# First batch's first DFT on quarters of the TensorE array, its input in halves from two queues, and a new order around it

## The chip, the cores and the metric

The kernel runs on one core of one Trainium2 chip. The metric is the device time of one execution in microseconds (us). Before the change it was 2508.93 us, the median of three runs (2508.61 to 2509.11).

## What is computed

The input x holds 8 batches of 3008 time steps by 256 channels. Each batch goes through a real FFT over time, a complex linear layer with biases, a soft threshold and the inverse FFT. Every time step then goes through a feed-forward block with a hidden width of 2048.

```
X = np.fft.rfft(x, axis=1)
Yr = Xr @ w_r - Xi @ w_i + b_r
Yi = Xr @ w_i + Xi @ w_r + b_i
Y  = sign(Y) * max(abs(Y) - 0.01, 0)
y  = np.fft.irfft(Y, n=3008, axis=1)
h  = y @ w_in
out = (h - tanh(h)) @ w_out
```

## The kernel before, in words

3008 is 64 times 47, so the FFT is done as two short DFTs by matmul: a **first DFT** over 47 points for each of 64 residues, and a **second DFT** over the 64 residues. Between the two the data goes through DRAM (`a_dram`), because the second needs rows of all residues together. After the linear layer and the threshold an inverse DFT over 64 points is written to DRAM (`z_dram`) and read back for the last inverse DFT of 47 points, which `Wave.time` does. The feed-forward block (`Chunk.up`, `Chunk.down`) then runs in 48 chunks of time steps. Batches 1 to 7 are transformed in the gaps of the feed-forward work of the batch ahead of them. Only batch 0 has nothing to hide behind, so the program begins with a stretch in which it is transformed alone. Everything below lies in this stretch.

**First DFT of batch 0** (class `Forward`). x comes in eight chunks of 96 partitions by 4 pairs of residues by 256 channels (384 KB), issued on the SP queue (L262). A chunk holds two residues one above the other, so 94 rows are in use; the rest of the 128 partitions is set to zero on POOL (L261), and the constant `f1` is block diagonal. Each chunk has two matmuls of 128 by 128 by 512 columns in float32 (L269), 16 in all. Each result is copied from PSUM to `st` by ACT or DVE in turn (L281). The 32 rows that the first units need go to DRAM first (`store_near`, L286), the other 64 later (`store_far`, L290).

**Second DFT to inverse DFT of batch 0** (class `WholeSpectrum`). There are 12 units, u0 to u11, of two frequencies each. A unit reads its rows from DRAM (L360), is transformed (L378), copied by ACT (`xf`, L477), summed by DVE (`sum`, `sf`, L482), multiplied with the linear layer (`cross`, L490 and L500; `cross_apart` for u11, L510 and L512), blended (`y`, L429), thresholded (L523, L527, L540) and inverted (L548). The units run as a software pipeline: pass i of a loop holds the transform of unit i, the cross products of unit i-1, the threshold of unit i-2 and the inverse of unit i-3.

**The weights of the linear layer** (`load_linear`, L142 to L149) are read between chunks 5 and 6 of x and combined on DVE and POOL (L155 to L165). The cross products need the result. **The feed-forward weights** come as 64-bit words and are taken apart into floats on DVE, ACT and POOL, in blocks. Six blocks, b0 to b5, are spread over the passes of the loop by two tables, `on_act` and `on_dve`, and each has steps named `exponent`, `mantissa`, `ends`, `fraction`, `scale`, `value` and `parts`.

**Filling** matmuls on zeros (`keep_warm`, L699) run ahead of the first DFT (8) and behind it (25).

The order on each engine is the order in which the program is written. Transfers of all queues take eight counters in turn, called DMAHW0 to DMAHW7 in the rows below. A transfer waits on its issuing engine until the one that took its counter before, eight transfers earlier, has landed.

Of the kernel before, what the change touches and what calls it, by code (L numbers as in the profile page):

```python
# [10 lines left out]
F32 = mybir.dt.float32  # L11
# [6 lines left out]
NP, NJ, GB = 32, 24, 5  # L18
# [14 lines left out]
def dft_constants():  # L33
# [6 lines left out]
    for par in range(2):  # L40
        plain[47 * par:47 * par + 47, 48 * par:48 * par + 48] = one
    by_pair = plain.reshape(94, 4, NJ // 2, 2).transpose(0, 2, 1, 3).reshape(94, 96)
    f1 = np.zeros((128, 2, 128))
    for half in range(2):
        f1[32 * half:32 * half + 94, half, :96] = by_pair
    f1 = f1.reshape(128, 256)
    f1s = np.zeros((94, 2, 48))
# [30 lines left out]
@with_exitstack  # L78
def spectral_ffn(ctx, tc, x, w_r, w_i, b_r, b_i, w_in, w_out, x_twice, b_turned, f1, f1s, f2, i1, i2, out):
    nc = tc.nc  # L80
# [58 lines left out]
    def load_linear():  # L139
        wr = ffn.tile([P, 2, D], F32, name="wr_f", tag="g_h")  # L140
        wi = load.tile([P, 2, D], F32, name="wi_f", tag="at", bufs=3)
        nc.sync.dma_start(out=wr, in_=w_r.rearrange("(t p) e -> p t e", p=P))  # L142
        nc.sync.dma_start(out=wi, in_=w_i.rearrange("(t p) e -> p t e", p=P))
        rows = load_bias(work.tile([33, 2, D], F32, name="bias_rows", tag="tmp", bufs=4), 33)
        return wr, wi, rows

    def load_bias(dst, n):
        for k, v in enumerate((b_r, b_i)):
            nc.sync.dma_start(out=dst[:, k, :], in_=v.rearrange("(o e) -> o e", o=1).to_broadcast([n, D]))  # L149
        return dst  # L150

# [86 lines left out]
    PAIRED, LOOK = 1, 4  # L238
    NEAR = 32
    stack = {}  # L240

    class Forward:
        def __init__(self, b, ch):
            self.b, self.ch = b, ch
            self.x, self.ps = {}, {}

        def load(self):
            if self.ch == 0:
                if self.b < PAIRED:
                    a_dram[self.b] = [dram.tile([NP, n, D], F32, name=f"a_{n}") for n in (NEAR, 96 - NEAR)]  # L250
                else:
                    a_dram[self.b] = dram.tile([2 * NP, 96, D], F32, name=f"a_{self.b}", tag="a_two")
            pool, tag = (load, "xt")
            if self.b == 0:
                pool, tag = ((load, "xt"), (load, "zin"), (work, "yh"), (work, "yl"))[self.ch // 2]
            elif self.ch >= 2:
                pool, tag = ((work, "yh"), (work, "yl"))[self.ch - 2]
            self.xt = pool.tile([P if self.b == 0 else 96, XC, D], F32, name="xt", tag=tag)
            lo = 32 * (self.ch % 2) if self.b == 0 else 0
            if self.b == 0:  # L260
                nc.gpsimd.memset(self.xt[:32] if lo else self.xt[96:], 0.0)  # L261
            nc.sync.dma_start(out=self.xt[lo:lo + 96], in_=x[self.b, :, self.ch * XC:(self.ch + 1) * XC, :])  # L262

        def whole(self, q):
            k, m = (P, P) if self.b == 0 else (94, 96)
            self.ps[q] = ps_f.tile([P, 512], F32, name="ps_f1", tag="f")
            pv = self.ps[q][:m].rearrange("p (a d) -> p a d", d=D)
            lo = self.ch % 2 * P
            nc.tensor.matmul(pv, stack["whole"] if self.b else f1f[:, lo:lo + m], self.xt[:k, 2 * q:2 * q + 2, :], start=True, stop=True)  # L269

        def keep(self, q, copy=nc.scalar.copy):
            n = 2 if self.b and self.ch >= 2 else XC
            if n == 2:
                self.st = ffn.tile([96, 2, D], F32, name="st", tag=("th", "g")[q])
            elif q == 0:
                pool, tag = (work, "st")
                if self.b == 0 and self.ch >= 2:
                    pool, tag = ((load, "xt"), (load, "zin"), (work, "yh"))[self.ch // 2 - 1]
                self.st = pool.tile([96, XC, D], F32, name="st", tag=tag)
# [4 lines left out]
        def store_near(self, q=0, n=XC):  # L284
            p = self.ch * XC + 2 * q
            nc.sync.dma_start(out=a_dram[0][0][p:p + n].rearrange("a r d -> r a d"), in_=self.st[:NEAR, 2 * q:2 * q + n])  # L286

        def store_far(self):
            p = self.ch * XC
            nc.sync.dma_start(out=a_dram[0][1][p:p + XC].rearrange("a r d -> r a d"), in_=self.st[NEAR:])  # L290

# [46 lines left out]
    def rows(parts, jp):  # L338
        late = 8 * jp >= NEAR
        t = parts[late].rearrange("a (q g e) d -> a q g (e d)", g=4, e=2)  # L340
        return t[:, jp - late * NEAR // 8]

# [347 lines left out]
    with tc.manual_schedule(engines={E.PE, E.Activation, E.DVE, E.Pool, E.SP}):  # L690
        zero = cvt.tile([P, 512], F32, name="zero", tag="w_f")
        nc.vector.memset(zero, 0.0)
# [3 lines left out]
        def keep_warm(n):  # L696
            idle = ps_h.tile([P, 512], F32, name="idle", tag="h")
            for _ in range(n):
                nc.tensor.matmul(idle, warm[:, :P], warm, start=True, stop=True)  # L699
# [4 lines left out]
        f1f = load_whole(f1, [P, 2 * P], "f1")  # L704
        first = [Forward(0, ch) for ch in range(NP // XC)]
# [5 lines left out]
        steps = [(f, q) for f in first for q in range(XC // 2)]  # L711
        for i in range(len(steps) + 1):
            if i < len(steps):
                steps[i][0].whole(steps[i][1])
            if i >= 1:
                f, q = steps[i - 1]
                f.keep(q, nc.vector.tensor_copy if i % 2 == 0 else nc.scalar.copy)
                if f is first[-1]:
                    f.store_near(q, 2)
                elif q == 1:  # L720
                    f.store_near()
                    if 4 <= f.ch < 7:
                        first[f.ch - 4].store_far()
# [24 lines left out]
        def unit(i):  # L748
# [66 lines left out]
        u11.threshold()  # L815
        for op in (b4.scale, b5.fraction, b5.scale):
            op()
# [17 lines left out]
        forward(0)  # L835
        forward(1)
        for k in range(5):
            keep(k)
            forward(k + 2)
            if k == 1:  # L840
# [7 lines left out]
        b4.value()  # L848
        keep(5)
        following[2].store()  # L850
        b5.value()
        keep(6)
        following[3].store()
        b4.parts()
        b5.parts()
        p, q = blocks[:2]
# [154 lines left out]
```

## Time and profile before

| | |
|---|---|
| median of three runs | 2508.93 us |
| profiled execution, its own time | 2506.88 us |
| its span in the trace | 2505.1 us |
| PE busy | 2488.9 us (99% of the span) |
| PEld busy | 2232.6 us (89%) |
| DVE busy | 1864.7 us (74%) |
| ACT busy | 1511.9 us (60%) |
| POOL busy | 114.5 us (5%) |

The span runs from the first to the last instruction, and the profiled execution is 1.78 us longer than it. PE's share is an average: filling matmuls on zeros count as busy too, and in the first 100 us PE waits for other work in several places.

### The profile page before, as it was taken

Reading aid. Unit: us, or ns where it says so; the run is one execution under the profiler, and the core shown is the slowest. Engines: PE = TensorE matmul, PEld = TensorE weight load, DVE = VectorE, ACT = ScalarE, POOL = GpSimd, SP = SyncE. Lnnn points to the kernel's source line nnn. Section 1 sums busy time; section 2 is a strip of 40 time slices with the busy share of each in tenths; the row PEclk is TensorE's granted clock in tenths of the full one; section 3 lists DMA queues with packets and bytes.
Section 4 is the critical chain, followed back from the end, with each engine's and each line's share of the span. In section 5 each row is a group of like instructions: output and inputs, shape, how many; then the busy total and the mean of one; then the engine's idle time right before and its main releaser. Section 6 shows DMA issues by size and latency. Waiting matters only on the chain.

```text
span 2505.1 us, 36438 instructions
## 1 busy us (share of the span) xinstructions
PE 2488.9 (99%) x13330; PEld 2232.6 (89%) x13330; DVE 1864.7 (74%) x3411; ACT 1511.9 (60%) x2930; POOL 114.5 (5%) x116
## 2 busy tenths in 40 slices
PE   9999999999999999999999999999999999999999
PEld 6789998999989999899988999889998899988888
DVE  5896887677776777777777777767777677765655
ACT  4676558555685556855577555775557655555554
POOL 2110000000001000010000000000000000000000
PEclk9999999999999999999999999999999999999999
DMA  8544227332363223633146221553216522010000
GB/s 245 180 113 127 76 68 209 90 76 62 85 188 88 70 59 90 190 80 79 43 138 165 71 74 40 152 152 78 67 39 169 133 69 63 28 51 17 20 17 17
DMA packets 156446, 236.57 MB, mean 94 GB/s; under 512 B 12498, under 2 KB 107498, under 8 KB 156266
## 3 DMA queue, kind: packets, MB, share of 16 engines
q1 hardware_dynamic: 144937, 213.78, 29.4%
q0 software_dynamic: 11328, 20.45, 5.4%
q8 instruction: 105, 1.72, 0.3%
q14 instruction: 76, 0.61, 0.1%
HBM read 138.77 MB, written 95.42 MB: 93 GB/s over the span
## 4 chain that ended last, share of the span: by engine, by line
PE 91%; DVE 5%; DMA 1%; ACT 1%; issue 1%; SPq 0%; DVEq 0%; ACTq 0%
PE o L667 37%; PE h L634 37%; PE ps_v L398 4%; PE ps_i L590 4%; PE ps_f L378 3%; PE ps_t L398 2%; PE ps_f L318 2%; DVE y L429 1%; PE ps_i L445 1%; PE ps_i L446 1%; PE ps_i L444 1%; DVE gl L654 1%; DVE g L648 1%; DMA xt<-in_x 1%; DMA xt<-in_x_twice 1%
## 5 line engine op out<-in xcount | busy, mean ns | idle before, releaser
L648 DVE TENSOR_TENSOR g<-h,th 128x502 f32<-128x502 f32 (+2 forms) x768 | 520.4, 678 | 289.1 <-ACT th L645 283.1
L645 ACT ACTIVATE th<-h 128x502 f32<-128x502 f32 (+2 forms) x768 | 452.0, 589 | 448.2 <-PE h L634 443.6
L654 DVE TENSOR_TENSOR gl<-g,gh 128x502 fp32r<-128x502 f32 (+2 forms) x768 | 524.0, 682 | 257.2 <-ACT gh L651 246.7
L651 ACT CAST gh<-g 128x502 fp32r<-128x502 f32 (+2 forms) x768 | 469.7, 612 | 356.2 <-DVE g L648 354.2
L667 PE MATMUL o<-gh,wout_l 128*128 128x502 f32 (+2 forms) x1536 | 584.9, 381 | 0.6 <-DVE ot L684 0.2
L667 PE MATMUL o<-gl,wout_h 128*128 128x502 f32 (+2 forms) x1536 | 576.9, 376 | 0.6
L667 PE MATMUL o<-gh,wout_h 128*128 128x502 f32 (+2 forms) x1536 | 576.3, 375 | 0.0
L634 PE MATMUL h<-yh,win_l 128*128 128x502 f32 (+2 forms) x1536 | 454.2, 377 | 1.4 <-DVE g L648 0.9
L634 PE MATMUL h<-yl,win_h 128*128 128x502 f32 (+2 forms) x1536 | 450.6, 375 | 0.0
L634 PE MATMUL h<-yh,win_h 128*128 128x502 f32 (+2 forms) x1536 | 450.2, 375 | 0.0
L634 PEld LDWEIGHTS h<-yh,win_l 128*128 128x128 f32 x1536 | 287.6, 188 | 44.0 <-DVE g L648 4.9
L667 PEld LDWEIGHTS o<-gl,wout_h 128*128 128x128 f32 x1536 | 289.7, 189 | 38.6 <-DVE gl L654 3.4
L634 PEld LDWEIGHTS h<-yl,win_h 128*128 128x128 f32 x1536 | 290.1, 189 | 34.8 <-DVE yl L626 0.4
L634 PEld LDWEIGHTS h<-yh,win_h 128*128 128x128 f32 x1536 | 290.2, 189 | 34.3
L667 PEld LDWEIGHTS o<-gh,wout_l 128*128 128x128 f32 x1536 | 290.7, 189 | 31.0 <-DVE ot L684 2.7
L667 PEld LDWEIGHTS o<-gh,wout_h 128*128 128x128 f32 x1536 | 290.8, 189 | 28.0
L365 POOL DMA_DIRECT2D at<-a x84 | 80.0, 1031 | 1873.1 <-DMA at<-a 931.5
L429 DVE TENSOR_TENSOR y<-tb,ps_v 64x256 f32<-64x256 f32 x384 | 160.2, 417 | 6.1 <-ACT tb L516 2.2
L313 DVE TENSOR_TENSOR xs<-xt,xs 47x512 fp32r<-47x512 f32 x208 | 138.4, 681 | 25.8 <-ACT xs L312 24.1
L312 ACT CAST xs<-xt 94x512 fp32r<-94x512 f32 x208 | 125.6, 625 | 6.4 <-DMA xt<-in_x_twice 6.3
L321 ACT COPY st<-ps_f 96x512 f32<-96x512 f32 x208 | 116.1, 579 | 1.4 <-PE ps_f L318 1.3
L625 ACT CAST yh<-yt 128x470 fp32r<-128x470 f32 (+36 forms) x200 | 87.0, 460 | 49.4 <-DVE yt L606 29.3
(113 smaller groups left out, 2488.9 us busy)
## 6 DMA issues: line engine op xcount, KB each, us to landing
xt<-in_x_twice SPq DMA_DIRECT2D x104, 384.0 KB
a<-st SPq DMA_DIRECT2D x104, 384.0 KB
at<-a SPq DMA_DIRECT2D x96, 256.0 KB
z<-zo SPq DMA_DIRECT2D x93, 240.0 KB
zin<-z SPq DMA_DIRECT2D x46, 480.0 KB
at<-a POOLq DMA_DIRECT2D x72, 256.0 KB, 5.0
out<-ot SPq DMA_DIRECT2D x29, 502.0 KB
turn<-in_i SPq DMA_DIRECT2D x96, 128.0 KB
```

What stands on the lines that cost most here:

```text
L312: nc.scalar.copy(out=xs, in_=src)
L313: nc.vector.tensor_tensor(out=xs[:47], in0=src[:47], in1=xs[:47].bitcast(F32), op=ALU.subtract)
L321: nc.scalar.copy(out=self.st[:, 2 * q:2 * q + 2, :], in_=ps[:96].rearrange("p (a d) -> p a d", a=2))
L398: nc.tensor.matmul(paired(dst, D), lhs[:, t], in_turn(rhs[:, t, :]), start=n == 0, stop=n == 5)
L429: nc.vector.tensor_tensor(out=y[ri * 64:(ri + 1) * 64, jj, :], in0=common(jj, ri), in1=self.side(ri)[jj * 64:(jj + 1) * 64], op=ALU.add,)
L590: nc.tensor.matmul(ps[:, at:at + m], self.zt[:m, k, t * P:(t + 1) * P], i2t[:m, turn:turn + m], start=True, stop=True,)
L634: nc.tensor.matmul(paired(h, n), lhs[:, t, f * P:(f + 1) * P], moving(rhs[:, t], n), start=k == 0, stop=k == 5,)
L645: nc.scalar.activation(out=th[:, :n], in_=h[:, :n], func=AF.Tanh)
L648: nc.vector.tensor_tensor(out=g[:, :n], in0=h[:, :n], in1=th[:, :n], op=ALU.subtract)
L651: nc.scalar.copy(out=gh[:, :n], in_=g[:, :n])
L654: nc.vector.tensor_tensor(out=gl[:, :n], in0=g[:, :n], in1=gh[:, :n].bitcast(F32), op=ALU.subtract)
L667: nc.tensor.matmul(paired(self.o[t], n), lhs[:, f, t * P:(t + 1) * P], in_turn(rhs[:, :n]), start=f == 0 and k == 0, stop=f == NF - 1 and ...
```

## The change

The first DFT of batch 0 gets a class of its own, `First`, and x of batch 0 a tensor of its own, `x_first`, with the two residues of a pair apart. A chunk goes to partitions 0 to 47 by SP's queue and to partitions 64 to 111 by ACT's queue. Each chunk has four matmuls of 47 rows by 64 columns of weights by 512 columns, each on another quarter of the array; 32 in all in place of 16. ACT copies the results of one half of the rows, DVE of the other. The zeros on POOL are gone. `f2` and the weights of the linear layer are read by ACT's queue, the latter behind its copies of the DFT. The near and far stores become 16 each, of half the size. Three units read their rows ahead of the far stores, not two. In the last pass the sum of u11 is put ahead of the threshold of u9, and steps of b4 and b5 move from the loop to behind it.

```diff
+    class First:
...
+            for h, queue in enumerate((nc.sync, nc.scalar)):
+                queue.dma_start(out=self.xt[64 * h:64 * h + 48], in_=x_first[h, :, self.ch * XC:(self.ch + 1) * XC, :])
+
+        def dft(self):
+            self.ps = [ps_f.tile([P, 512], F32, name="ps_f1", tag="f") for _ in range(2)]
+            for h, q in ((0, 0), (1, 1), (0, 1), (1, 0)):
+                rows = slice(64 * h, 64 * h + 47)
+                out = self.ps[h][64 * q:64 * q + 64].rearrange("p (a d) -> p a d", d=D)
+                nc.tensor.matmul(out, f1t[rows], self.xt[rows, 2 * q:2 * q + 2, :], start=True, stop=True)
+
+        def keep(self):
...
+            for h, copy in enumerate((nc.scalar.copy, nc.vector.tensor_copy)):
+                copy(out=self.st[:, :, h], in_=self.ps[h].rearrange("p (a d) -> p a d", d=D))
+
+        def store(self, part):
+            lo, hi = ((0, NEAR), (NEAR, 48))[part]
+            for q in range(2):
+                n = self.ch * XC + 2 * q
+                dst = a_dram[0][part][n:n + 2].rearrange("a h r d -> r (a h) d")
+                nc.sync.dma_start(out=dst, in_=self.st[64 * q + lo:64 * q + hi].rearrange("r a h d -> r (a h) d"))
...
-        keep_warm(8)
+        keep_warm(7, zero[:, :P], zero[:, :P])
...
-            if f.ch == 6:
-                lin_in = load_linear()
             f.load()
-        f2t = load_const(f2, [P, 384], "f2")
+        f2t = const.tile([P, 384], F32, name="f2")
+        nc.scalar.dma_start(out=f2t, in_=f2)
+        for f in first:
+            f.dft()
+            f.keep()
+            f.store(0)
+        lin_in = load_linear(nc.scalar)
         bias = const.tile([P, 2, D], F32, name="bias")
-        keep_warm(25)
+        keep_warm(27)
         units = [WholeSpectrum(0, jp) for jp in range(NJ // 2)]
-        for u in units[:2]:
+        first[0].store(1)
+        for u in units[:3]:
             u.load()
-        for f in first[3:]:
-            f.store_far()
-        units[2].load()
+        for f in first[1:]:
+            f.store(1)
...
-            9: [b2.parts], 10: [b3.parts, b4.ends], 11: [b5.ends],
+            9: [b2.parts], 10: [b3.parts, b4.ends],
...
-            10: [b5.exponent, b5.mantissa, b4.fraction],
...
+            if i + 1 == NU:
+                unit(i).sum()
             if unit(i - 2):
                 unit(i - 2).shrink()
-            unit(i).sum()
+            if i + 1 < NU:
+                unit(i).sum()
...
-        for op in (b4.scale, b5.fraction, b5.scale):
+        for op in (b5.exponent, b5.mantissa, b4.fraction, b4.scale, b4.value):
             op()
```

ACT's queue at the start of the program, before, where `st` is the copy of a DFT result (PE_49 counts PE's work):

```order
L281 ACT_TABLE_LOAD
L281 COPY st<-ps_f_141 96x512 [waits PE_49]
L281 COPY st<-ps_f_147 96x512 [waits PE_49]
L281 COPY st<-ps_f_155 96x512 [waits DMAHW1_49,PE_49]
L281 COPY st<-ps_f_163 96x512 [waits DMAHW2_49,PE_49]
```

And the same place with the change:

```order
L247 DMA xt<-in_x_first 48x1024 x4
L247 DMA xt<-in_x_first 48x1024 [waits DMAHW1_49]
L247 DMA xt<-in_x_first 48x1024 [waits DMAHW3_49]
L247 DMA xt<-in_x_first 48x1024 [waits DMAHW5_49]
L247 DMA xt<-in_x_first 48x1024 [waits DMAHW7_49]
L714 DMA f_132<-in_f 128x384 [waits DMAHW1_49]
L260 ACT_TABLE_LOAD
L260 COPY st<-ps_f_134 128x2x256 [waits PE_49]
L260 COPY st<-ps_f_145 128x2x256 [waits PE_49]
```

Nine transfers now stand ahead of ACT's table load and its first copy. The second row that waits for DMAHW1, `f2`, waits for the ACT half of chunk 4, which holds that counter by then (numbered from 0, chunk 4 is the fifth).

SP's queue behind the DFT with the change, where a_106 takes the near rows and a_107 the far rows; the rows begin with the near stores of chunk 5:

```order
L267 DMA a_106<-st 16x4x256 [waits DMAHW0_49,DVE_49,Activation_49]
L267 DMA a_106<-st 16x4x256 [waits DMAHW1_49]
L267 DMA a_106<-st 16x4x256 [waits DMAHW2_49,DVE_49,Activation_49]
L267 DMA a_106<-st 16x4x256 [waits DMAHW3_49]
L267 DMA a_106<-st 16x4x256 [waits DMAHW4_49,DVE_49,Activation_49]
L267 DMA a_106<-st 16x4x256 [waits DMAHW5_49]
L267 DMA a_107<-st 32x4x256 [waits DMAHW6_49]
L267 DMA a_107<-st 32x4x256 [waits DMAHW7_49]
L364 DMA at<-a_106 128x1x512 [waits DMAHW3_49,DMAHW4_49,DMAHW2_49,DMAHW5_49,DMAHW1_49,DMAHW0_49]
L364 DMA at<-a_106 128x1x512 x2
L267 DMA a_107<-st 32x4x256 x3
```

And ACT's queue at the same place, where `wr`, `wi` and the two rows of biases take the counters 1, 3, 4 and 6:

```order
L260 COPY st<-ps_f_211 128x2x256 [waits DMAHW4_49,DMAHW3_49,PE_49]
L140 DMA wr_f<-in_w_r 128x2x256 [waits DMAHW1_49]
L141 DMA wi_f<-in_w_i 128x2x256 [waits DMAHW3_49]
L144 DMA bias_rows<-in_b_r 33x256 [waits DMAHW4_49]
L144 DMA bias_rows<-in_b_i 33x256 [waits DMAHW6_49]
```

The second near store of chunk 5 waits for DMAHW1, now held by `wr`, which ACT issues behind its last copy of the DFT; the stores of chunks 6 and 7 behind it wait for `wi` and the first row of biases, and the first far store for the second row. The reads of u0, u1 and u2 (L364) stand behind them all.

DVE in the last two passes of the loop, before (sf is `sum`, y the blend, L205, L220 and L223 the steps of b5 and b4):

```order
L540 TENSOR_TENSOR mn<-up,mn 128x512 [waits DVE_49,Activation_49]
L205 TENSOR_SCALAR w_s<-w_raw 128x512 [waits DMAHW5_49]
L220 TENSOR_SCALAR w_m<-w_raw 128x512
L223 SCALAR_TENSOR_TENSOR w_f<-w_raw,w_m 128x512 [waits Pool_49]
L429 TENSOR_TENSOR y<-tb_755,ps_v 64x256 [waits PE_49,Activation_49]
L429 TENSOR_TENSOR y<-tb_755,ps_v 64x256 x3
L527 TENSOR_SCALAR mn<-y 128x512 [waits DVE_49,PE_49]
L482 TENSOR_TENSOR sf<-ps_f_757,xf 128x256 [waits Activation_49]
L540 TENSOR_TENSOR mn<-up,mn 128x512 [waits DVE_49,Activation_49]
```

And with the change:

```order
L544 TENSOR_TENSOR mn<-up,mn 128x512 [waits DVE_49,Activation_49]
L486 TENSOR_TENSOR sf<-ps_f_785,xf 128x256 [waits Activation_49]
L433 TENSOR_TENSOR y<-tb_783,ps_v 64x256 x4
L531 TENSOR_SCALAR mn<-y 128x512 [waits DVE_49]
L544 TENSOR_TENSOR mn<-up,mn 128x512 [waits DVE_49,Activation_49]
```

Three steps of the weight blocks are gone from between u8 and u9, and the sum of u11 has moved ahead of the blend of u9.

## Rows read from the trace of the kernel before

**Rows 1.** The page: the shares by engine of the chain that ended last.

```profile
PE 91%; DVE 5%; DMA 1%; ACT 1%; issue 1%; SPq 0%; DVEq 0%; ACTq 0%
```

**Rows 2.** The chain that ended last, in order of time: start us, us, what.

```profile
28.32 3.56 DMA at<-a
...
35.97 0.89 PE ps_f L378 x8
...
183.78 1.00 PE o L667 x5
```

**Rows 3.** Timeline of SP's queue: start, us, line, transfer, count.

```profile
1.20 2.80 SPq L262 DMA_DIRECT2D xt<-in_x  x6
4.05 0.61 SPq L142 DMA_DIRECT2D wr_f<-in_w_r  x1
...
6.80 0.31 SPq L149 DMA_DIRECT2D bias_rows<-in_b_i  x1
8.39 1.85 SPq L262 DMA_DIRECT2D xt<-in_x  x2
11.49 0.36 SPq L131 DMA_DIRECT2D f<-in_f  x1
...
20.51 1.06 SPq L286 DMA_DIRECT2D a<-st  x2
23.03 1.24 SPq L360 DMA_DIRECT2D at<-a  x2
24.31 3.91 SPq L290 DMA_DIRECT2D a<-st  x5
```

**Rows 4.** Timeline, PE: start, us, line, output and inputs, count, idle before.

```profile
2.04 3.78 PE L699 MATMUL idle<-warm 128*128 128x512 f32 x8 [2.04 <-DVE column L703]
...
5.61 10.54 PE L269 MATMUL ps_f<-xt,f_f 128*128 128x512 f32 x24
...
16.70 3.67 PE L269 MATMUL ps_f<-xt,f_f 128*128 128x512 f32 x8 [0.55 <-DMA xt<-in_x]
...
19.80 6.29 PE L699 MATMUL idle<-warm 128*128 128x512 f32 x25
...
26.25 2.02 PE L378 MATMUL ps_f<-f,at 128*128 128x128 f32 x16 [0.15 <-issue]
...
32.01 1.13 PE L378 MATMUL ps_f<-f,at 128*128 128x128 f32 x8 [0.92 <-DMA at<-a]
```

**Rows 5.** Windows of 2 us: busy time by engine, granted clock, DMA share, GB/s.

```profile
4.00:6.00 2.00, 2.00 (x6) 1.43 (x5) 0.00 (x0) 0.00 (x0) 1.89 (x3) 1.00 1.07 268
...
18.00:20.00 2.00, 2.00 (x7) 0.95 (x5) 0.69 (x1) 0.86 (x2) 0.00 (x0) 1.00 1.09 379
...
36.00:38.00 2.00, 2.00 (x14) 1.84 (x13) 1.90 (x4) 1.42 (x3) 1.03 (x1) 1.00 1.03 390
```

**Rows 6.** Timeline, ACT and DVE in the first DFT.

```profile
0.75 1.28 ACT L281 ACT_TABLE_LOAD   x1 [0.75 <-PEq L981]
...
6.74 0.58 ACT L281 COPY st<-ps_f 96x512 f32<-96x512 f32 x1 [4.71 <-PE ps_f L269]
...
7.60 0.69 DVE L281 COPY st<-ps_f 96x512 f32<-96x512 f32 x1 [5.60 <-PE ps_f L269]
```

**Rows 7.** Timeline, the last two passes over the units, and a copy behind them.

```profile
77.15 0.60 ACT L477 COPY xf<-ps_f 128x512 f32<-128x512 f32 x1
77.26 0.44 DVE L205 TENSOR_SCALAR w_s<-w_raw 128x512 uint32<-128x512 uint32 x1
...
77.94 0.70 DVE L223 SCALAR_TENSOR_TENSOR w_f<-w_raw,w_m 128x512 f32<-128x512 uint32 x1
...
78.54 1.71 DVE L429 TENSOR_TENSOR y<-tb,ps_v 64x256 f32<-64x256 f32 x4
...
81.29 1.13 PE L512 MATMUL ps_t<-wr_f,sf 128*128 128x256 f32 x4 [2.41 <-DVE sf L482]
...
90.85 0.69 DVE L281 COPY st<-ps_f 96x512 f32<-96x512 f32 x1 [1.03 <-PE ps_f L269]
```

More of the change, by code (lines that the diff above doesn't have):

```diff
@@ L41, in dft_constants @@
         plain[47 * par:47 * par + 47, 48 * par:48 * par + 48] = one
[L42 to L46, printed above, removed]
+    by_unit = one.reshape(47, 2, NJ // 2, 2).transpose(0, 2, 1, 3).reshape(47, 48)
+    f1 = np.zeros((128, 64))
+    f1[:47, :48] = f1[64:111, :48] = by_unit
     f1s = np.zeros((94, 2, 48))
@@ L137, in load_whole, with load_linear @@
         return t
-    def load_linear():
+    def load_linear(queue):
         wr = ffn.tile([P, 2, D], F32, name="wr_f", tag="g_h")
[L141 to L144, printed above, removed]
+        wi = ffn.tile([P, 2, D], F32, name="wi_f", tag="g_l")
+        queue.dma_start(out=wr, in_=w_r.rearrange("(t p) e -> p t e", p=P))
+        queue.dma_start(out=wi, in_=w_i.rearrange("(t p) e -> p t e", p=P))
+        rows = work.tile([33, 2, D], F32, name="bias_rows", tag="tmp", bufs=4)
+        for k, v in enumerate((b_r, b_i)):
+            queue.dma_start(out=rows[:, k, :], in_=v.rearrange("(o e) -> o e", o=1).to_broadcast([33, D]))
         return wr, wi, rows
[L147 to L150, printed above, removed]
     def combine_linear(wr, wi, rows, zero):
@@ L244, in __init__, with keep @@
             self.b, self.ch = b, ch
-            self.x, self.ps = {}, {}
+            self.ps = {}
         def load(self):
             if self.ch == 0:
[L249 to L262, printed above, removed]
+                a_dram[self.b] = dram.tile([2 * NP, 96, D], F32, name=f"a_{self.b}", tag="a_two")
+            pool, tag = ((load, "xt"), (load, "xt"), (work, "yh"), (work, "yl"))[self.ch]
+            self.xt = pool.tile([96, XC, D], F32, name="xt", tag=tag)
+            nc.sync.dma_start(out=self.xt, in_=x[:, self.ch * XC:(self.ch + 1) * XC, :])
         def whole(self, q):
-            k, m = (P, P) if self.b == 0 else (94, 96)
             self.ps[q] = ps_f.tile([P, 512], F32, name="ps_f1", tag="f")
[L267 to L272, printed above, removed]
+            pv = self.ps[q][:96].rearrange("p (a d) -> p a d", d=D)
+            nc.tensor.matmul(pv, stack["whole"], self.xt[:94, 2 * q:2 * q + 2, :], start=True, stop=True)
+        def keep(self, q, copy):
+            n = 2 if self.ch >= 2 else XC
             if n == 2:
@@ L275, in keep @@
             elif q == 0:
[L276 to L279, printed above, removed]
+                self.st = work.tile([96, XC, D], F32, name="st", tag="st")
             p = 2 * q % n
@@ L338, in rows @@
     def rows(parts, jp):
[L339 to L341 removed]
+        late = 4 * jp >= NEAR
+        t = parts[late].rearrange("a h (q i e) d -> (a h) q i (e d)", i=2, e=2)
+        return t[:, jp - late * NEAR // 4]
     def halves(t, jp):
@@ L691, in spectral_ffn, with keep_warm @@
         zero = cvt.tile([P, 512], F32, name="zero", tag="w_f")
-        nc.vector.memset(zero, 0.0)
+        nc.vector.memset(zero[:, :P], 0.0)
+        nc.vector.memset(zero[:, P:], 0.0)
         warm = work.tile([P, 512], F32R, name="warm", tag="sp_h", bufs=3)
         nc.vector.tensor_copy(out=warm, in_=zero)
-        def keep_warm(n):
+        def keep_warm(n, lhs=warm[:, :P], rhs=warm):
             idle = ps_h.tile([P, 512], F32, name="idle", tag="h")
             for _ in range(n):
-                nc.tensor.matmul(idle, warm[:, :P], warm, start=True, stop=True)
@@ L701, in spectral_ffn @@
-        keep_warm(8)
+                nc.tensor.matmul(idle[:, :rhs.shape[-1]], lhs, rhs, start=True, stop=True)
+        keep_warm(7, zero[:, :P], zero[:, :P])
         for k, v in enumerate((-LAM, 1150 * 2.0**23, 254 * 2.0**23)):
             nc.vector.memset(column[:, k:k + 1], v)
-        f1f = load_whole(f1, [P, 2 * P], "f1")
-        first = [Forward(0, ch) for ch in range(NP // XC)]
+        f1t = load_whole(f1, [P, 64], "f1")
+        first = [First(ch) for ch in range(NP // XC)]
         for f in first:
-            if f.ch == 6:
-                lin_in = load_linear()
@@ L709, in spectral_ffn @@
             f.load()
-        f2t = load_const(f2, [P, 384], "f2")
[L711 to L723, printed above, removed]
+        f2t = const.tile([P, 384], F32, name="f2")
@@ L839, in spectral_ffn @@
             forward(k + 2)
+            if k == 0:
+                b5.fraction()
+            if k == 2:
+                b5.scale()
+                b4.parts()
             if k == 1:
```

31 lines of the change are left out of this document (18 added, 13 removed).

## The prediction

> **What bounds the kernel now.** First the page's own chain by engine: 91% of the way to the end runs over PE [rows 1]. Next the chain in order of time, to see where that holds. From 183.78 us on it is feed-forward matmuls of PE and little else [rows 2], so anything saved or lost before then moves the whole rest, and anything else in the program hides behind PE. The change touches only the stretch before 100 us, so the question is by how much the first feed-forward matmul moves. In that stretch the chain is mixed: transfers of x, PE in the first DFT, transfers through DRAM, then ACT and DVE in the units. Third came the queue and engine timelines, which give the first stretch its times. SP issues x from 1.20 us. The waits in its queue end when the transfer eight places earlier lands, so its issues at 6.80, 8.39 and 11.49 us date the landing of chunks 1, 2 and 4 [rows 3]. That is one chunk of 384 KB each 1.56 us, or 252 GB/s; the engines that move it are full (DMA share 1.07 from 4 to 6 us) [rows 5]. PE begins the DFT at 5.61 us, is late once by 0.55 us for chunk 6, which the weights of the linear layer were put ahead of, and hands over to the filling at 19.80 us [rows 4]. The last near stores are issued by 21.57 us, u0's read at 23.03, and its second DFT starts at 26.25 [rows 3, 4]. That last time, and what follows from it, is what I move.
>
> The profiled execution took 2506.88 us, 2.05 below the median of the runs shown. I work out a shift in the trace and add it to the median, 2508.93.
>
> **The change, step by step.**
>
> *x.* The bytes are the same. `f1` shrinks from 128 to 32 KB ahead of it, worth 0.39 us at 252 GB/s, and the weights no longer stand before chunk 6. Chunk 0 landed 1.56 before chunk 1, at 5.24; now at 4.85, and chunk k at 4.85 + 1.56k: chunk 2 at 8.0, 4 at 11.1, 7 at 15.8. The rate through two queues is not in the trace: the low end is what x shows now, the high end the 390 GB/s of other loads from 36 to 38 us [rows 5]. I take 252, since the same rows go to nearly the same partitions, and the 16 engines are already full.
> The Trainium skill, "DMA: Bandwidth & Descriptors", section "Rules for kernel authors", says of two transfers to disjoint partition halves not to bother, since both share the same engines. By that the sum below stands; by the 390 of the row it would be that of the third rival. No row shows a second queue beside SP's in this stretch, so the trace does not decide it.
>
> *ACT's queue.* This is the dearest side effect. ACT issues half of x and then `f2`, which waits for chunk 4's half: 11.1 us. Its issue is 0.36 [rows 3], then the table load, 1.28, which before ran at 0.75 us beside nothing [rows 6]. ACT's first copy so starts at 12.75 instead of 6.74. PSUM has four buffers for the DFT. Chunks 0 and 1 fill them; DVE empties two, for chunk 2; chunk 3 needs both of ACT's first copies, 2 x 0.6: 13.95 us.
>
> *The DFT.* One old matmul is two records, 24 and 8 of them for the 16 matmuls; the first 24 begin within 5.61 to some 16 us, 0.43 apart [rows 4], thus 0.86 for one matmul. A row of results is now four matmuls on four quarters. If the quarters run together, a chunk costs 0.86. Five chunks behind 13.95 end at 18.25, ACT's last copy at 18.85. PE stands idle between chunk 2 (ready by 8.9) and 13.95. Its granted clock reads 1.00 all through, but the first eight filling matmuls came 0.43 us apart and the 25 later ones 0.25 [rows 4]: 512 columns in 0.43 is 1.2 GHz, so PE began at the lower of its two levels, after idling. After the 2.41 us of idling before 81.29 it did not fall: four records in 1.13 [rows 7]. Five us lies between; the price is 0 to 1.7 (two chunks at double time). I take 1.7, as the start is the only row of a long idle: ACT is done at **20.55**.
>
> *From there to u0.* ACT issues `wr` (0.61), then `wi` and the two rows of biases, three more issues of 0.31 to 0.61, together 1.2. A 256 KB read took at most 3.2 us from issue to use (23.03 to 26.25) [rows 3, 4]: `wr` lands 3.2 after ACT is done, the rest by 4.4. SP's last five near stores wait for these one after another, so the last is issued at about 4.4. It lands 1.46 later (21.57 to 23.03), and u0's read takes 3.2: 9.1 in all, u0 at **29.65**, against 26.25: **+3.4**. If the small transfers land sooner it is 1 us less; if they queue behind the far stores, 1 more. The combination of the weights on DVE and POOL lies in the wait for u0's read, and the 27 filling matmuls (6.8 us) end before it.
>
> *u2 and u3.* Before, u2's read stood behind five far stores (3.91 us of issue [rows 3]) and landed 3.56 after 28.32, at 31.88 [rows 2], when PE had waited 0.92 us for it [rows 4]. Now it goes ahead of them: **-0.9**. Instead 14 far stores of half the size stand before u3's read: 14 x 0.39 by the 3.91 for five, 5.5 us. It is issued some 7.4 after u0's and can be used at 10.6. u3 began 9.7 after u0 before (35.97 against 26.25 [rows 2, 4]), 12.9 after u0's read and 12.0 without u2's wait, so it is in time by 1.4; no cost, up to +1 if the queue is slow.
>
> *The last unit.* DVE sets the pace there. Three steps (77.26 to 78.64) leave the place before u9's blend; the sum of u11 enters it and has to wait for `xf`, done at 77.75 [rows 7]. The blend starts at 78.2 in place of 78.54; with what follows it is **-0.45**, bounds 0 and -1.3. PE's wait of 2.41 us before 81.29 goes, but u11's inverse still waits for DVE's two later blends. The steps moved behind it run while z makes its way through DRAM; DVE stood idle for 1.03 us between two copies there [rows 7], and I cost them at nothing. If that cover failed they would cost up to 1.3.
>
> The zeros on POOL were beside the loads: nothing. Sum: 3.4 - 0.9 - 0.45 = **+2.05**, 2508.93 + 2.05 = **2511**.
>
> **The rivals.**
>
> *Two at a time, slower.* An old matmul is two records, the second behind the first on the same weights' place. If PE starts records strictly in turn, the second record of one quarter holds up the first of the next quarter until it starts itself; two quarters overlap and never four. Then a record costs 0.43 and a chunk of eight records half of 8 x 0.43, 1.71 us: as much as the old DFT. Five chunks from 13.95 end at 22.95 with the last record's overhang, ACT at 23.55 (25.25 with the slow clock): 4.7 more, 2515.7, or 2514 with the clock up. It decides as soon as a chunk takes over 1.5 us. For it: the two records [rows 4]. Against it: nothing in this trace, which has no matmul on part of the array in both directions.
> The Trainium skill, "TensorE: Matmul & The Clock Gate", section "Part 3: Packing small matmuls — row/col tiling", says that matmuls start and end in program order, which leads to this rival; the same section has 16 tiles of single-pass matmuls gain over tenfold, which leads to the forecast. No run here shows either.
>
> *The quarters don't overlap.* The change then doesn't do what it says: a chunk costs 4 x 0.86 = 3.42, eight from 4.85 end at 32.2, ACT at 32.8: 12.3 over the forecast, 2523.
>
> *x comes faster by two queues.* At 390 GB/s a chunk is 1.01 us. From a start near 3.16 us (5.24 less 512 KB at 252) chunk 4 lands at 8.3, ACT starts at 9.95, chunk 3 at 11.15, and ACT is done at 16.05 to 17.75: 2.8 to 4.5 under the forecast, 2506.5 to 2508.2. For it: 379 GB/s from 18 to 20 us with loads and stores mixed [rows 5].
>
> **How the numbers follow.** Forecast 45%, two at a time 32%, no overlap 8%, faster x 12%, others 3%. A measurement of this kernel tells about 0.2%, 5.0 us, from no change. The forecast and the faster x lie within that; of two at a time some 30% does, with the clock up or the smaller waits; a gain beyond 5 us needs all the low bounds at once. So same 0.62, slower 0.34, faster 0.04. The range reaches from the faster x, 2506.5, to two at a time with its bound of 1 us, 2517; it leaves out no overlap and little else.
>
> **What would show it.** In the new profile: PE's records of the DFT, 64 of them, four at once if the chunks step by 0.86; ACT's table load at about 11.5 us and not at 0.75; a gap of about 5 us on PE after chunk 2; SP's near stores of chunks 5 to 7 waiting for `wr`, `wi` and the biases; u0's second DFT at 29.7 instead of 26.25, and no wait for u2. The prediction is wrong if ACT copies before 10 us, if chunks step by 1.7 us or more, or if u0 starts before 27 us.

## The result, and the profile after

The changed kernel takes 2522.33 us (median of 6 runs, 2521.91 to 2523.89) against 2508.28 (6 runs, 2507.38 to 2509.11) for the kernel before beside it: 1.0057 of it, interval 1.0044 to 1.007. That is slower by 14.0 us, outside the range of 2506.5 to 2517, where I had forecast 2511 and "no change" as likeliest. The profiled execution took 2522.66 us, 0.33 over the median.

The program as a whole is what it was: the shares by engine of the chain that ended last answer to [rows 1].

```profile
PE 91%; DVE 5%; DMA 2%; ACT 1%; issue 1%; SPq 0%; DVEq 0%; ACTq 0%
```

The timeline of PE of the changed kernel, to be laid beside [rows 4]:

```profile
1.06 3.35 PE L704 MATMUL idle<-zero 128*128 128x128 f32 x14 [1.06 <-DVE zero L696]
5.59 1.09 PE L254 MATMUL ps_f<-xt,f_f 47*64 47x512 f32 x8 [1.18 <-DMA xt<-in_x_first]
...
9.09 1.21 PE L254 MATMUL ps_f<-xt,f_f 47*64 47x512 f32 x8 [0.86 <-DVE st L260]
12.98 9.29 PE L254 MATMUL ps_f<-xt,f_f 47*64 47x512 f32 x40 [2.68 <-ACT st L260]
22.20 8.00 PE L704 MATMUL idle<-warm 128*128 128x512 f32 x27
32.56 3.59 PE L382 MATMUL ps_f<-f,at 128*128 128x128 f32 x16 [2.37 <-issue]
...
93.60 1.10 PE L552 MATMUL ps_i<-mn,turn 128*128 128x256 f32 x4 [1.06 <-issue]
...
106.07 2.02 PE L284 MATMUL ps_f<-xt,f1s_f 94*96 94x512 f32 x2 [6.21 <-ACT st L293]
```

Read three things in it. A chunk of the new DFT is one bundle of 8 records in 1.09 us: four matmuls that would take 0.86 each alone, so the quarters do run together. But the last five chunks take 9.29 us, and the 27 filling matmuls behind them 8.00, where 25 took 6.29 before. And there is a wait of 6.21 us at 106, in the first DFT of batch 1. Before, its 14 matmuls came in one piece, right behind the last inverse (87.14):

```profile
88.08 6.17 PE L269 MATMUL ps_f<-xt,f1s_f 94*96 94x512 f32 x14
...
97.91 0.84 PE L634 MATMUL h<-yh,win_l 128*128 128x470 f32 x2
```

The first of the losses is in the granted clock (windows of 2 us; behind the busy times stand the clock, DMA's share and GB/s):

```profile
8.00:10.00 2.00, 1.14 (x12) 0.36 (x8) 0.69 (x1) 0.00 (x0) 0.00 (x0) 1.00 1.05 227
...
12.00:14.00 2.00, 1.02 (x5) 0.63 (x9) 0.00 (x0) 1.89 (x4) 0.00 (x0) 0.50 1.03 231
...
20.00:22.00 2.00, 2.00 (x12) 0.33 (x4) 0.69 (x1) 0.59 (x1) 0.00 (x0) 0.50 0.25 40
...
26.00:28.00 2.00, 2.00 (x11) 1.64 (x9) 2.00 (x3) 0.62 (x1) 1.79 (x1) 1.00 0.83 135
```

From 11.96 to 25.61 us TensorE ran at the lower of its two levels (0.50, that is 1.2 GHz). ACT's timeline gives the pace, since it copies one half of each chunk:

```profile
10.65 0.36 ACTq L714 DMA_DIRECT2D f<-in_f  x1
11.04 1.28 ACT L260 ACT_TABLE_LOAD   x1 [11.04 <-DMA xt<-in_x_first]
12.34 1.56 ACT L260 COPY st<-ps_f 128x512 f32<-128x512 f32 x3
15.48 0.59 ACT L260 COPY st<-ps_f 128x512 f32<-128x512 f32 x1 [1.58 <-PE ps_f L254]
17.19 0.59 ACT L260 COPY st<-ps_f 128x512 f32<-128x512 f32 x1 [1.12 <-PE ps_f L254]
...
22.31 0.59 ACT L260 COPY st<-ps_f 128x512 f32<-128x512 f32 x1 [1.12 <-PE ps_f L254]
```

The table load sits at 11.04 and not at 0.75 [rows 6], and the copies then come 1.71 us apart, which is the pace of the old DFT at the full clock (16 matmuls of 0.86 in 8 chunks). The chain that ended last shows what follows, and the second loss:

```profile
12.98 9.34 PE ps_f L254 x40
22.32 2.79 DMA wr_f<-in_w_r
25.12 0.30 SPq L267
...
26.88 2.10 DMA a<-st
29.05 0.64 SPq L364
...
100.31 0.39 SPq L300
...
100.75 4.58 DMA a<-st
...
105.44 0.59 ACT st L293
```

A near store in SP's queue waits for `wr`, whose issue by ACT stood behind the last copy; u0's read goes out at 29.05 (23.03 before, [rows 3]), and its DFT begins at 32.56 instead of 26.25. Far behind, at 100.75, a copy of batch 1's first DFT waits for the store of an earlier one. PE stands still meanwhile, and the clock is at 0.50 again from 104.12 to 110.94 us. The first feed-forward matmul comes at 112.84 instead of 97.91.

So of 14.9 us at that point, 6.3 are there at u0, 6.5 at the last unit's inverse (93.60 against 87.14), and 8.5 more come between it and the feed-forward: 6.2 of wait, and 2.3 that lie mostly in the lower clock behind it (the matmuls of L594 take 5.20 us there, 3.80 in run 1 below).

### The profile page after: what moved, and what is told of

Same layout as the page of the kernel before. It is cut to its first block, busy times and chain, and to the rows that moved or that the text cites. A ratio compares the mean times of both kernels' runs of the same rounds, so it can differ in the third digit from the quotient of the medians.

```text
span 2520.9 us, 36532 instructions
## 1 busy us (share of the span) xinstructions
PE 2493.3 (99%) x13370; PEld 2236.4 (89%) x13370; DVE 1864.5 (74%) x3412; ACT 1510.4 (60%) x2930; POOL 107.2 (4%) x108
## 4 chain that ended last, share of the span: by engine, by line
PE 91%; DVE 5%; DMA 2%; ACT 1%; issue 1%; SPq 0%; DVEq 0%; ACTq 0%
PE o L671 37%; PE h L638 36%; PE ps_v L402 4%; PE ps_i L594 4%; PE ps_f L382 3%; PE ps_t L402 2%; PE ps_f L322 2%; DVE y L433 1%; PE ps_i L450 1%; PE ps_i L449 1%; PE ps_i L448 1%; DVE gl L658 1%; DVE g L652 1%; DMA xt<-in_x_twice 1%; DMA xt<-in_x_first 0%
```

## The experiments

The kernel before ran beside all of them, with medians of 2507.46 to 2507.84. All runs in one table (the DFT of u0 and the first feed-forward matmul are starts in the profiled execution):

| run | u0's DFT | first feed-forward | median us | ratio to before, 95% |
|---|---|---|---|---|
| before | 26.25 | 97.91 | 2508.28 | |
| changed | 32.56 | 112.84 | 2522.33 | 1.0057 (1.0044, 1.007) |
| 1, b5.scale early | 33.58 | 106.11 | 2515.39 | 1.0028 (1.0018, 1.0038) |
| 2, end of the batch as before | 32.51 | 105.88 | 2515.51 | 1.003 (1.002, 1.0041) |
| 3, ACT free early | 33.14 | 113.93 | 2523.94 | 1.0062 (1.0047, 1.0077) |
| 4, filling after chunk 2 | 30.84 | 111.35 | 2521.49 | 1.0054 (1.0037, 1.0071) |
| 5, full start filling | 32.52 | 114.59 | 2521.75 | 1.0056 (1.0041, 1.0071) |
| 6, issues moved | 29.11 | 101.07 | 2512.44 | 1.0019 (1.001, 1.0028) |
| 7, and full start filling | 30.07 | 102.14 | 2511.58 | 1.0016 (1.0006, 1.0025) |
| 8, and filling between chunks | 29.09 | 101.61 | 2511.85 | 1.0019 (1.0009, 1.0029) |
| 9, stores on GpSimd | 27.84 | 100.69 | 2508.85 | 1.0005 (0.9996, 1.0014) |
| 10, no far store ahead | 26.83 | 99.79 | 2509.77 | 1.0014 (1.0005, 1.0023) |
| 11, weights early, old end | 27.23 | 100.43 | 2509.49 | 1.0013 (1.0004, 1.0022) |
| 12, weights early, new end | 26.91 | 99.99 | 2508.45 | 1.0001 (0.9993, 1.001) |

### 1 and 2: the wait at 106 us

Blocks b4 and b5 of the feed-forward weights keep their raw data in the two `st` buffers of `work`. `b5.scale` is the last reader of b5's, and the change moved it behind the third copy of batch 1's first DFT. That copy then can't have b5's buffer and takes the other one, which holds a result until its store has landed. Run 1 moves one line, run 2 puts the whole end of the batch back:

```diff
             if k == 0:
                 b5.fraction()
+                b5.scale()
             if k == 2:
-                b5.scale()
                 b4.parts()
```

> The changed kernel with one step moved back: b5.scale, the last reader of a weight block that lies in a buffer of the tile st, stands before the third copy of batch 1's first DFT and not behind it. Theory (buffer): that copy has to take the other st buffer only because b5's is still in use, and so waits for a store to land. Then the wait of 7.7 us of ACT on a<-st goes, the first feed-forward matmul comes at about 105 us in place of 112.84, and the time is 2514 (2513 to 2515.5). Rival (round trip): the read back of z or the weight blocks hold that place, and the copy's wait only hides it: the first feed-forward matmul stays above 110 us, time 2520 to 2523.

> The changed kernel with the whole end of the units stage (last sum, steps of b4 and b5) as it was before; the first DFT stays changed. Buffer theory: the same gain as by the one step, less the 0.3 to 0.5 us that the new order was worth up to u11's inverse: 2514.3 (2513.3 to 2516). Then what is left against before, 5.5 to 6.5 us, is the first DFT's part. Rival (round trip): above 2520, as the place is held by something that began in the first 60 us.

Run 1 took 2515.39, 6.9 less than the change, and its PE timeline has the 14 matmuls in one piece again:

```profile
95.57 6.17 PE L284 MATMUL ps_f<-xt,f1s_f 94*96 94x512 f32 x14
102.55 3.80 PE L594 MATMUL ps_i<-i,zin 120*128 120x120 f32 x32 [0.80 <-DVE st L293]
```

From the last inverse (94.64) to the first feed-forward matmul it now takes 11.5 us, where the change took 19.2 and the kernel before 10.8; u0 happened to come 1.0 later in this trace. One line's place is worth half of the loss, which settles the buffer theory. Run 2 is as fast (2515.51): beside the repaired line, the rest of the new order is worth nothing that the medians show. In the traces the new order gains in one place and loses in the next. From u0 to the last inverse run 2 takes 63.0 us and run 1 61.1; from there to the feed-forward run 2 takes 10.4 and run 1, with a wait of 0.80 for a copy, 11.5. What run 2 lost in the last unit is a matmul's wait of 2.41 us, which is back with the old order, and this time the clock fell in it, at 88.16 (timeline and window, PE alone):

```profile
88.51 2.07 PE L516 MATMUL ps_t<-wr_f,sf 128*128 128x256 f32 x4 [2.41 <-DVE sf L486]
```

```profile
88.00:90.00 2.00, 1.49 (x4) 0.54 0.87 241
```

The same four records took 1.13 us in the trace of before, after the same wait [rows 7].

### 3 to 5: why the clock is low in the DFT

Three edits of the changed kernel, each alone. Run 3 lets ACT issue only the halves of chunks 0 to 3, and SP the other halves and `f2`. Run 4 fills the gap with matmuls. Run 5 gives the start its eight matmuls of 512 columns back.

```diff
-            for h, queue in enumerate((nc.sync, nc.scalar)):
+            for h, queue in enumerate((nc.sync, nc.scalar if self.ch < 4 else nc.sync)):
...
-        nc.scalar.dma_start(out=f2t, in_=f2)
+        nc.sync.dma_start(out=f2t, in_=f2)
```

```diff
             f.dft()
+            if f.ch == 2:
+                keep_warm(11)
             f.keep()
```

```diff
-        keep_warm(7, zero[:, :P], zero[:, :P])
+        keep_warm(8)
```

> The changed kernel with ACT's queue relieved: ACT issues its halves of chunks 0 to 3 only, SP the rest of x and f2, so that ACT's table load and first copy no longer wait for chunk 4. The tail with its wait stays. Theory A (idling): PE's clock fell because PE stood idle from 10.4 to 13.0 us; without the idle stretch it stays at 1.00, the chunks step by x's 1.56 us, ACT is done by 17.5, u0 starts at 26.5 to 27.5, time 2517 (2516 to 2518). Theory B (quarters): matmuls on quarters do not hold the clock, idle or not; it falls within the DFT, the last chunks take 1.71 us each, u0 starts at 28 to 29.5, time 2518.5 (2517.5 to 2520), and the granted clock reads 0.50 in the last part of the DFT although PE never waited over 1 us.

> The changed kernel with eleven filling matmuls on the whole array put behind chunk 2 of the DFT, in PE's idle stretch from 10.4 to 13.0 us; ACT stays as late as it is. Theory A (idling): the clock stays at 1.00, the last five chunks take 0.86 us each and end at 17.5, u0 starts at about 28, time 2518 (2517 to 2519). Theory B (quarters): the clock holds through the filling and falls behind it, while the quarters are at work from 13 us on; chunks step by 1.71 at the end, u0 starts at 30 to 32, time 2520 to 2522.5.

> One edit to the changed kernel: the filling at the start is again eight matmuls of 512 columns, as before, in place of seven of 128. Theory A (TensorE's clock falls because PE idles behind ScalarE's late copies, 2.6 us before chunk 3): the idle is still there, the last five chunks again take 1.71 us each, the filling behind them 8 us, and the time stays near 2522 (2520 to 2524). Theory B (pairs of quarters cannot hold the clock at the rate at which x lands): the same 2522. Theory C (the shorter start leaves TensorE at the lower level when the DFT begins): the chunks take about 1.1 us each to the end, the copies end near 20.0 instead of 22.9, and the time is about 2518.

In run 3 ACT copies from 7.48 us on and PE's row shows no wait in the DFT, yet the copies are 1.71 apart again (once 2.80), and the time, 2523.94, is above what either theory gave:

```profile
5.46 15.03 PE L254 MATMUL ps_f<-xt,f_f 47*64 47x512 f32 x64 [1.04 <-DMA xt<-in_x_first]
20.42 7.64 PE L704 MATMUL idle<-warm 128*128 128x512 f32 x27
33.14 3.55 PE L382 MATMUL ps_f<-f,at 128*128 128x128 f32 x16 [5.08 <-issue]
```

So idling behind ACT, my reason for the clock's price, is not needed for the low pace. The granted-clock column reads 1.00 all through this DFT, but it knows no level ahead of the trace's first record of the clock. That record is a rise to 1.00, at 5.76 us in the kernel before, at 5.13 in the changed one and only at 23.11 in run 3. Run 3 thus doesn't show a fall. It shows that TensorE was low from the start, that 15 us of quarters didn't bring it up, and that the rise came in the full-array filling behind them. Run 4 shows the quarters at the other level:

```profile
5.57 6.50 PE L254 MATMUL ps_f<-xt,f_f 47*64 47x512 f32 x24 [1.15 <-DMA xt<-in_x_first]
12.00 3.69 PE L704 MATMUL idle<-warm 128*128 128x512 f32 x11
15.62 4.92 PE L254 MATMUL ps_f<-xt,f_f 47*64 47x512 f32 x40
```

Three chunks take 6.50 us, then eleven full-array matmuls run, in which the clock rises (13.95), and the five chunks behind them take 4.92, with copies 0.96 apart on average (16.76 to 20.58). Four quarters at the full clock are thus 1.8 times as fast as the old DFT, and at the lower level just as fast. The pace came out as in theory A, the time (2521.49) as in theory B, since a near store waited for `wi` until 25.1 us and u0's read went out at 27.70. Run 5 changed nothing in the time (2521.75): the shorter start (theory C) is not what slowed the last five chunks. And it shows the fall by itself (timeline and window, PE alone):

```profile
9.44 1.96 PE L254 MATMUL ps_f<-xt,f_f 47*64 47x512 f32 x8 [0.61 <-DMA xt<-in_x_first]
13.20 9.29 PE L254 MATMUL ps_f<-xt,f_f 47*64 47x512 f32 x40 [1.80 <-ACT st L260]
```

```profile
10.00:12.00 2.00, 1.40 (x8) 0.50 1.04 256
```

The clock rose at 6.55 us, in the first chunk, and fell at 9.96, in the third, before PE's wait for ACT began. In the changed kernel it fell at 11.96, within that wait.

Why did run 3 not profit from copies that ended 1.8 us earlier? SP issued its near stores until 27.8 us, because they waited for the linear weights, which ACT issued from 20.5 us on and which take counters that both queues share:

```profile
20.97 3.20 DMA wi_f<-in_w_i
24.20 0.30 SPq L267
...
27.82 2.11 DMA a<-st
30.01 0.61 SPq L364
```

### 6 to 8: the repairs together

Run 6 is run 3 with `b5.scale` early and the linear weights issued by SP right behind `f2`. Run 7 adds the full start filling, run 8 also two filling matmuls behind each of the first seven chunks. Shown here are the weights' move (run 6) and the filling between the chunks (run 8).

```diff
...
         nc.sync.dma_start(out=f2t, in_=f2)
+        lin_in = load_linear(nc.sync)
         for f in first:
             f.dft()
+            if f.ch < 7:
+                keep_warm(2)
             f.keep()
             f.store(0)
-        lin_in = load_linear(nc.scalar)
```

> Three repairs together: the last eight halves of x, f2 and the linear weights are issued by SyncE (so ScalarE copies from 7.5 us on and no near store waits for a transfer issued late), and b5.scale stands early (no buffer wait in batch 1's first DFT). The earlier run with the first of these alone had the DFT end at 20.5 with every chunk at 1.71, and its stores then lost 5 to 7 us to the linear weights' transfers. Expected here: DFT end 20.5, first unit's read issued at 24.5 to 25.5, its DFT at 28 to 28.9 (before: 26.25), no stall at 105, and the time 2509.5 to 2511. If the stores were not held by those transfers, the first unit stays near 33 and the time near 2515.

> The same with the start filling of before (eight of 512 columns). Theory B: the chunks fall to 1.71 each as soon as they come one by one with x (1.56 us apart); DFT end 20.5, time 2509.5 to 2511, the same as with the short start. Theories A and C: no idle and a full start, so the chunks stay at 1.1 and follow x; DFT end near 17, the first unit's DFT at 24 to 25, and the time 2505 to 2507.

> The same again with two filling matmuls of 512 columns behind each of the first seven chunks (0.5 us each chunk at the full clock), so that TensorE works on the whole array between the quarters. Theory B: the clock stays up, the chunks take about 1.1, DFT end near 17 to 17.5, the first unit's DFT at 24 to 25.5, the time 2505 to 2507, faster than the same without them by 3 to 5. If filling does not help: chunk and filling at half speed take 1.71 plus 0.85 each, DFT end near 25 and the time 2514 or more.

Windows of run 7, where ACT is free, the start full, and nothing between the chunks:

```profile
8.00:9.00 1.00, 0.70 (x8) 1.00 1.06 205
9.00:10.00 1.00, 0.42 (x4) 0.61 1.09 164
10.00:12.00 2.00, 2.00 (x12) 0.50 1.00 215
```

and of run 8:

```profile
10.00:12.00 2.00, 2.00 (x14) 1.00 1.05 254
...
28.00:30.00 2.00, 0.92 (x4) 0.66 0.83 264
```

With quarters alone, one bundle at a time as x lands, the clock falls at 9.22 us, with no wait between bundles over 0.87; with full-array matmuls between them it is never below 1.00 in the DFT, and each chunk takes 1.09 (one 1.21). So the filling holds the clock up. Whether the fall comes of the quarters or of the short waits between the bundles, which the filling shortens too, is not shown: no run has full-array matmuls with such waits. What speaks for the quarters is that without any wait they didn't raise the clock either, in the 9.29 us of the changed kernel. In time, all three runs missed: run 6 is 1.4 above its range, run 7 a little above that of theory B (2511.58), and run 8, for which I expected 2505 to 2507, is no faster than run 6 (2511.85 and 2512.44). Its DFT ends at 19.4 and u0 still begins at 29.09. SP shows why:

```profile
15.49 9.66 SPq L267 DMA_DIRECT2D a<-st  x18
25.94 1.92 SPq L364 DMA_DIRECT2D at<-a  x3
```

Eighteen stores, 0.54 us apart on average, stand between the last load and u0's read; the change has two near stores for each chunk, where all but the last had one, and SP could begin them only behind the weights' issue at 14.65. PE idles from 25.8 to 29.1, and the clock falls there (0.66), so that u0 and u1 take 3.44 us instead of 2.02.

### 9 to 12: is there a version that wins?

From here on GpSimd's own queue, which has its own counters, issues the second near store of each chunk, `f2` and the linear weights; two filling matmuls stand behind the first five chunks. Run 10 also drops the far stores ahead of u0's read. Runs 11 and 12 bring `f2` and the weights forward behind the fourth and fifth chunk, share the far stores between the two queues, combine the weights ahead of them and have 31 filling matmuls; 11 has the old end of the batch, 12 the new one.

```diff
-                nc.sync.dma_start(out=dst, in_=self.st[64 * q + lo:64 * q + hi].rearrange("r a h d -> r (a h) d"))
+                (nc.gpsimd if q and part == 0 else nc.sync).dma_start(out=dst, in_=self.st[64 * q + lo:64 * q + hi].rearrange("r a h d -> r (a h) d"))
```

> Built from the runs so far: x as in the previous repairs, two filling matmuls behind each of the first five chunks, the full start filling, b5.scale early; the second near store of each chunk, f2 and the linear weights are issued by GpSimd on its own queue and counters, so SyncE has one near store per chunk. Theory (SyncE's issues, 18 of 0.53 us from 15.5 us on, held the first unit's read to 25.9 while the copies were done at 20.1): DFT end 18 to 18.5, last near issue 19.5, first unit's read at 22.5 with the two far stores ahead of it, its DFT at 25.5 to 26, time 2507 to 2509. Rival: the path to the first unit is set by the stores' landing or by a slow GpSimd queue, read at 25 or later, time 2511 or more.

> The same with the two far stores of chunk 0 behind the reads of the first three units: first unit's read at 21.6 to 22, its DFT at 24.7 to 25.2, time 2505.5 to 2508 (before 2507.6), 1 lower than with them ahead. Rival: the third unit, or the fourth behind 16 far stores, waits for its read by what the first gained, and the time is the same as with them ahead. With a slow GpSimd queue 2510 or more.

> The last run's first unit waited for the biases' transfer, the last on GpSimd's queue (21.92 to 26.12, then ScalarE's cast). Here f2 goes out behind the fourth chunk and the linear weights and biases behind the fifth; the far stores are shared between SyncE and GpSimd behind the first three reads; the filling has 31 matmuls; and the end of the first batch is ordered as in the kernel before. Expected: first unit's read at 21.5, its DFT at 24.5 at the full clock (2.0 for the first two units), 1.7 ahead of before's 26.25; first feed-forward matmul at 96.2 (before 97.91); time 2505.8 to 2506.8, 0.9993 to 0.9997 of before. Rival: the transfers of the weights, now among the last chunks of x, delay x and the near stores by as much (0.58 MB), and nothing is won: 2507 to 2509.

> The same with the change's order of the end of the first batch, b5.scale early. In the last run its last inverse began at 87.93 and the first feed-forward matmul 11.86 later, with a wait of 1.18 for the last inverse's stored result; in the kernel before it was 10.77 later without such a wait. If the new order only moves the wait (from the linear product to the stored result), this run is 0 to 0.6 slower than the same with the order of before; if the sum put first is worth what the change meant, it is 0.5 or more faster.

Run 9 came to 2508.85, within what I expected of SP's issues as the limit, but with u0's read at 24.04 and its DFT at 27.84, 1.5 and 2 us later than I put them; that the time fits is partly luck. Run 10 did read u0 early, at 21.52, and then waited for something else (the chain); at 2509.77 it missed its range:

```profile
21.92 4.20 DMA bias_rows<-in_b_i
...
26.20 0.63 ACT bias_top L156
26.83 3.65 PE ps_f L382 x16
```

In runs 11 and 12 the weights were out of the way, but the near stores behind them on GpSimd's queue landed 2.7 to 3.2 us after their issue, and u0's read went out at 23.2 to 23.5, where it stood before the change. So the rival of run 11 came true: nothing was won, and its 2509.49 is above even the rival's range. Run 12's PE timeline shows where the new end stands:

```profile
26.91 1.13 PE L382 MATMUL ps_f<-f,at 128*128 128x128 f32 x8 [1.67 <-DMA at<-a]
...
41.35 1.10 PE L552 MATMUL ps_i<-mn,turn 128*128 128x256 f32 x4 [1.46 <-DMA turn<-in_i]
...
96.43 3.80 PE L594 MATMUL ps_i<-i,zin 120*128 120x120 f32 x32 [0.68 <-DMA zin<-z]
```

From u0 to the last unit's inverse it takes 61.7 us (run 11: 62.8, where the clock was at 0.50 from 83.41 to 86.82 us behind the wait of 2.39), with 1.46 of wait for `turn`, a constant of the inverse that SP reads behind the far stores; before the feed-forward 0.7 is lost again to the stored result. Run 12 is 1.04 below run 11 in the median, as expected if the new order is worth something. No version beats the kernel before; runs 9 and 12 can't be told from it. The repairs bring the loss from 14.0 us down to 1.0 (by the medians), and what quarters save in the DFT (its end at 17.9 in run 12, 20.4 before) does not reach u0, whose read goes out when the last near store has landed.

## Why the prediction was wrong

The two steps that failed:

- **The clock's price, "0 to 1.7", with 1.7 taken.** I put it at two chunks at double time after a long idle. All five chunks ran at 1.2 GHz, in 9.29 us where run 4 has 4.92 at the full clock: the price was 4.4, over my bound. Two smaller errors lie beside it: at the full clock five chunks take 0.6 more than my five times 0.86, and chunk 3 began 0.97 earlier than forecast. Together ACT was done at 22.90, not 20.55, 2.35 later. The reason I gave was not the needed one either: in the changed kernel the clock did fall within PE's wait, but in runs 5 and 7 it fell without such a wait, and in run 8, with matmuls on the whole array in between, it stayed up. And I didn't carry the clock on: u0 and u1 started at the lower level (32.44 to 35.85 us) and took 3.59 us instead of 2.02, which ate the 0.9 that u2 gained and 0.5 more.
- **"The steps moved behind it ... I cost them at nothing", at worst 1.3.** It was 8.5 us. I had counted the moved steps' own time and looked for cover for it, and did not ask which buffer they release. `b5.scale` is the last reader of a buffer that the next copy needs; moved behind that copy, it sends the copy to the other buffer and so makes it wait for a store's landing (run 1). The changed order could be read in advance: the third copies of batch 1's first DFT wait for transfers there, and did not before. Without this step the time would have been in the range, as run 1 is (2515.39).

The measured 2522.3 is near the 2523 of the rival without overlap, but that is chance: a chunk took 1.09 to 1.71 us here and never that rival's 3.42.

What held:

- **x through two queues** came at 239 and 233 GB/s (windows 5 to 10 and 10 to 15 us) where I took 252, and the third rival (390) fell. The rule of the Trainium skill that I weighed there ("DMA: Bandwidth & Descriptors", "Rules for kernel authors") agrees with these windows.
- **ACT's lateness**: first copy at 12.34, forecast 12.75; chunk 3 at 12.98 for 13.95. The gap on PE ahead of it was 2.68 us, not 5, since chunk 2 had ended only at 10.30.
- **The quarters overlap**: 8 records in 1.09 us, and 0.96 a chunk in a row, where I took 0.86. The rival of two at a time fell, though the five chunks of the trace step by its 1.71 us, which I had named as a sign of being wrong. That number alone would have confirmed the wrong theory; the granted clock beside it, and run 4 with 0.96 at the full clock, tell them apart. In the Trainium skill, "TensorE: Matmul & The Clock Gate", section "Part 3: Packing small matmuls — row/col tiling", both sentences stand that I set against each other; the measured one, packed matmuls gaining, is what these rows show for four quarters.
- **From the last copy to u0**: 9.66, forecast 9.1, by the waits for `wr` that I had named. u2 has no wait, as said. u3 has none either, though its read went out 9.4 us behind u0's and not 7.4: the 14 far stores took 7.36 us for my 5.5.
- **The last unit**: from u2 to the last inverse the changed kernel is 0.34 shorter (+6.80 to +6.46), forecast 0.45.

Put right, the sum is 2511 + 2.35 (ACT's last copy) + 0.56 (from there to u0) + 1.39 (u0 to u2, +0.49 for my -0.9) + 0.11 (last unit) + 8.47 (buffer) = 2523.9; it was 2522.3, beside a kernel before that had a median 0.65 lower than in the runs that I started from.

What stays open is whether quarters or short waits let the clock fall, and why with the same start it rose early in some traces and late in others. With the change's shorter start filling, the first rise came at 5.13 and 4.77 us in two traces (changed, run 1) and at 13.95 to 26.72 in four (runs 2, 3, 4 and 6). With the start filling of before it came between 4.76 and 7.52 us in all seven traces that have it (runs 5 and 7 to 12), as it did in the kernel before. The prediction gave the shorter start no term; in the trace of the changed kernel the clock was up by 5.13 us all the same. And the ratios of runs 9 to 12 lie within their intervals of each other, so which of their orders is best is not shown.

## What to carry to other kernels

When a step is moved, ask which buffer its instruction is the last to read, and who takes that buffer next; its own duration is the smaller part. Packing matmuls on quarters of the array paid only at the full clock here, and where they came one by one with the data, only full-array matmuls between them held it; read the pace from the engine that empties PSUM, and don't expect the faster DFT to shorten the program by itself (run 8). And count the issues: a DFT that is faster on PE gives nothing if its results leave in twice as many stores through a queue that other loads still hold.

## What was not expected of the hardware

- Bundles of four quarter matmuls that came with x (one in 1.6 to 2 us) saw the granted clock fall to 0.50, at 8.19 us in run 1 (in a wait of 1.48 for x), 9.22 in run 7, 9.96 in run 5 and 11.96 in the changed kernel; bundles back to back behind eleven full-array matmuls were at the full pace through all of their 4.9 us (run 4).
- At the lower level, quarters without a wait did not bring the clock up: 9.29 us in the changed kernel, where the rise came in the full-array filling behind them, at 25.61.
- Waits of 2.4 us ahead of the last unit's linear product left the clock up in the trace of before [rows 7]; it fell at 88.16 us, in that wait, in run 2, and at 83.41, right behind it, in run 11.
- GpSimd issues a store of 64 KB in 0.51 us, no slower than the 0.54 between SP's in run 8. u0's read went out 2.6 us behind the start of the last of them in run 10, and 3.0 and 3.4 behind it in runs 11 and 12.
